# Ten units' q, k and v in one stretch by way of DRAM, two attention units at once, weights in PSUM, adds on GpSimd

## The chip, the cores and the metric

The kernel runs on one core of one Trainium2 chip. The engines that matter here are TensorE (PE in the profile, with its weight loads as PEld), VectorE (DVE), ScalarE (ACT), GpSimd (POOL) and SyncE (SP), which issues every DMA. Each engine works through its own queue in order and waits on semaphores for the others. The metric is the device time of one execution in microseconds (us).

## The reference

x has 2048 rows of 640 numbers, in float32. One layer is computed:

```python
xn = layernorm(x)                                  # over the 640 columns
q, k, v = split(xn @ wqkv)                         # 32 heads of 20 columns each
# sliding, dilated attention: row s sees rows s, s-2, s-4, ... s-14 (8 places)
logits = einsum("bhsd,bhswd->bhsw", q, kg) * 20 ** -0.5   # places before row 0 masked
attn = softmax(logits)
o = einsum("bhsw,bhswd->bhsd", attn, vg)
s = o @ wo
g = silu(((xn @ w_gate) * (xn @ w_up)) @ w_down)   # w_gate, w_up: 640 x 1536
return x + s * g
```

All products are to hold float32 precision.

## The kernel before

Every matrix operand is split into a high and a low part, and a product is the sum of three products of parts (`mm3`, L91, and `ALL3`, L89). ScalarE makes the high part, and VectorE or GpSimd subtracts it from the raw numbers to make the low part (`split`, L84).

The rows are ordered so that 16 tiles of 128 rows hold the even rows first (8 tiles) and then the odd rows (8 tiles): a dilation of 2 becomes two independent halves. Within a half, partition p holds 8 neighbouring rows, so the 8 places that a row sees lie in the same partition or in the one before. k and v of a half are held with 7 extra rows in front (`EXT` = 15), and these are copied from the partition before by DMAs from SBUF to SBUF (L350 to L354).

The attention is cut into twelve **units**: six groups of heads (`GROUPS`: four of five heads, two of six) times the two halves. For a unit, `qkv(u, i)` (L337) computes tile i of its q, k and v: 15 products of 300 or 360 columns into one PSUM bank with the tag q, which has four banks. ScalarE moves the bank's content into the SBUF tiles kv (L348) and q (L349). The tile kv exists twice, one for each half.

`attention(u)` (L357) is the work of a unit on VectorE, written as a generator that hands over after each step with an estimated cost. For each pair of places, q is multiplied with k for two places at once (L380, 1600 or 1920 elements) and summed over the 20 columns of a head (L384). After the mask and the maximum (L388 to L391), ScalarE takes the exponential (L393), and VectorE sums and divides (L396 to L398). Then the weights are multiplied with v, two places at a time (L403), added up (L411), and the two halves of the sum are added into o (L414). SP writes o to DRAM (L419).

TensorE's other large share is the gate and up product. `gate_up(f, ch)` (L440) computes one **piece**: 15 products of 512 columns for gate into a bank with the tag g, 15 for up into a bank u (two banks each). ScalarE moves the gate bank into a tile gs (L451, two of them), VectorE multiplies the up bank with gs into hs (L462), and SP writes hs to DRAM (L466). There are 48 pieces: 12 blocks f of the 1536 columns times 4 chunks ch of 512 rows.

Engines follow the order in which the Python code issues instructions. `advance(budget)` (L424) decides where attention steps stand among TensorE's work: after each q/k/v tile and each half of a piece it gets a budget in estimated microseconds (1.9 or 2.28 for a tile, 3.25 for half a piece) and issues steps of the running generators until the budget is spent. In the main loop (L982) a unit's eight tiles of q, k and v are followed by three pieces; attention of the unit is put in the list after its tiles, and `drain` (L960) issues what is left of the unit before the last one. The weights of a group of heads have one buffer each for the high and low part (wqh, wql); they are replaced after each second unit (`split_wq`, L978, the low part on VectorE). The low parts of the gate and up weights are subtracted on GpSimd, each subtraction put behind a product of the attention (`some_beside`, L145, and `behind`, L151).

After the pieces come the output product of the attention (L830, L96) and the down product (L699), for which o and hs are read back from DRAM.

Of the kernel before, what the change touches and what calls it, by code (L numbers as in the profile page):

```python
# [11 lines left out]
F32 = mybir.dt.float32  # L12
F32R = mybir.dt.float32r
AF = mybir.ActivationFunctionType
# [5 lines left out]
P = 128  # L20
# [31 lines left out]
def kernel(  # L52
# [138 lines left out]

    def idle_product(n):

        nc.tensor.matmul(pt([P, n, P], "q", 4), ident, ident.unsqueeze(1).to_broadcast([P, n, P]), start=True,
                         stop=True)

    for n in (3, 3, 3, 1):
# [67 lines left out]
        for _ in range(len(halves) if n is None else n):  # L265
            halves.pop(0)()

    def trans(s, bank=("q", 4), parts=((0, 4), (4, KD)), later=False):
        hi, lo = xT_tile(s)
        for k0, k1 in parts:  # L270
            p = pt([P, k1 - k0, P], *(("q", 4) if k0 else bank))
# [27 lines left out]

    def spread(s0):  # L300

        p = pt([P, NQ, 2, TPC], "q", 4)
# [15 lines left out]


    UN = [(g, r) for g in range(len(GROUPS)) for r in range(DIL)]  # L320
    q_t, kv_t, kv_buf, kv_zero = {}, {}, {}, {}

    def begin_unit(u):
        g, r = UN[u]
        c = GROUPS[g] * DH
        q_t[u] = st([P, NE, c], "q", 2)
        if r not in kv_buf:
            kv_buf[r] = st([P, EXT * 2 * CMAX], "kv", 2)
            kv_zero[r] = 0
        kv_t[u] = kv_buf[r][:, :2 * EXT * c].rearrange("p (a e c) -> p a e c", a=2, c=c)  # L330
        if kv_zero[r] != GROUPS[g]:
            nc.gpsimd.memset(kv_t[u][0:1, :, 0:W - 1, :], 0.0)
            kv_zero[r] = GROUPS[g]

    ALL_RUNS = [(a, b, k) for a, b in ALL3 for k in range(KD)]

    def qkv(u, i, runs=ALL_RUNS, at=None, act=None):  # L337

        g, r = UN[u]
        c = GROUPS[g] * DH  # L340
        p = pt([P, 3 * c], "q", 4)
        t0 = (i % TPC) * P
        for n, (a, b, k) in enumerate(runs):
            if n == at:
                act()
            nc.tensor.matmul(p, xT[(r * NE + i) // TPC][a][:, k, t0:t0 + P], wq[g][b][:, k], start=n == 0,  # L346
                             stop=n == len(runs) - 1, skip_group_check=act is not None)
        nc.scalar.activation(kv_t[u][:, :, W - 1 + i, :], p[:, c:].rearrange("p (a c) -> p a c", a=2), AF.Copy)  # L348
        nc.scalar.activation(q_t[u][:, i, :], p[:, :c], AF.Copy)  # L349
        for i0, i1 in ((1, 5), (5, NE)):  # L350
            if i == i1 - 1:
                for p0, p1 in ((0, 112), (112, 127)):
                    nc.sync.dma_start(kv_t[u][p0 + 1:p1 + 1, :, i0 - 1:i1 - 1, :],
                                      kv_t[u][p0:p1, :, W - 1 + i0:W - 1 + i1, :])  # L354


    def attention(u):  # L357
        g, r = UN[u]
        nh = GROUPS[g]
        c = nh * DH  # L360
        q, kv = q_t[u], kv_t[u]
        pair, one, small = [(n + 155) / 950 for n in (2 * NE * c, NE * c, NE * nh * W)]
        lg = st([P, NE * nh, W], "lg", 2)
        e = st([P, NE * nh, W], "e", 1)
        yield 1.0

        def places(a, j):

            y = kv[:, a, j:j + NE, :].rearrange("p i c -> p (i c)")
            return bass.AP(y.tensor, y.offset, [y.ap[0], [c, 2], y.ap[1]])  # L370

        def pair_tile():
            return st([P, 2, NE * c], "t", 2)

        def heads(y):
            return y.rearrange("p a (n d) -> p a n d", d=DH)

        for j in PAIRS:
            t = pair_tile()
            nc.vector.tensor_mul(t, q.rearrange("p i c -> p (i c)").unsqueeze(1).to_broadcast([P, 2, NE * c]),  # L380
                                 places(0, j))
            some_beside(t)
            yield pair
            nc.vector.tensor_reduce(out=lg[:, :, j:j + 2].rearrange("p n a -> p a n"), in_=heads(t),  # L384
                                    op=ALU.add, axis=AX.X)
            yield pair
        m0 = lg[0:1].rearrange("p (i h) w -> p i h w", h=nh)
        nc.vector.tensor_add(m0, m0, mask.unsqueeze(2).to_broadcast([1, NE, nh, W]))  # L388
        sm = st([P, 2, NE * nh], "sm", 2)
        nc.vector.tensor_reduce(out=sm[:, 0, :], in_=lg, op=ALU.max, axis=AX.X)  # L390
        nc.vector.tensor_sub(lg, lg, sm[:, 0, :].unsqueeze(2).to_broadcast([P, NE * nh, W]))  # L391
        yield 3 * small
        nc.scalar.activation(e, lg, AF.Exp, scale=SCALE)  # L393
        finish_piece()
        yield small
        nc.vector.tensor_reduce(out=sm[:, 0, :], in_=e, op=ALU.add, axis=AX.X)  # L396
        nc.vector.reciprocal(sm[:, 1, :], sm[:, 0, :])
        nc.vector.tensor_mul(e, e, sm[:, 1, :].unsqueeze(2).to_broadcast([P, NE * nh, W]))  # L398
        yield 3 * small

        def weighted(j, t):
            pw = e[:, :, j:j + 2].rearrange("p n a -> p a n").unsqueeze(3).to_broadcast([P, 2, NE * nh, DH])
            nc.vector.tensor_mul(heads(t), pw, heads(places(1, j)))  # L403

        acc, t = pair_tile(), pair_tile()
        weighted(PAIRS[0], acc)
        yield pair
        for j in PAIRS[1:]:
            weighted(j, t)
            yield pair  # L410
            nc.vector.tensor_add(acc, acc, t)  # L411
            yield pair
        o = st([P, NE, c], "o", 1)
        nc.vector.tensor_add(o.rearrange("p i c -> p (i c)"), acc[:, 0, :], acc[:, 1, :])  # L414
        yield one
# [8 lines left out]
    def advance(budget):  # L424
        credit[0] += budget
        while running and credit[0] > 0:
            try:
                credit[0] -= next(running[0][1])
            except StopIteration:
                running.pop(0)  # L430
        if not running:
            credit[0] = 0

    credit = [0]
# [119 lines left out]
    def out_proj(s, n):  # L554
# [4 lines left out]
        p = pt([P, HALF], "q", 4)  # L559
# [129 lines left out]
    def product(m):  # L689
# [2 lines left out]
        place = "ACACABA"[j]  # L692
        new = j in (0, 1, 5)
        if new:
            bank[place] = pt([P, HALF], {"A": "q", "B": "g", "C": "u"}[place], {"A": 4, "B": 2, "C": 2}[place])
# [122 lines left out]
    def pair_product(p, j):  # L818
        place = "ACACABA"[j]
        new = j in (0, 1, 5)  # L820
        if new:
            bank[p, place] = pt([P, HALF], {"A": "q", "B": "g", "C": "u"}[place], {"A": 4, "B": 2, "C": 2}[place])
# [112 lines left out]
    gate_up(0, 2)  # L935
    trans_q(15)
    low_parts()
    running.append((0, attention(0)))
    for i in range(TPC, NE):
        qkv(1, i)  # L940
        advance(PACE * 1.9)
    running.append((1, attention(1)))
    split_wq(1, nc.gpsimd)
    gate_up(1, 2)
    gate_up(0, 3)
# [11 lines left out]
        if ch == 0:  # L957
            split_wf_beside(f + 1)

    def drain(u):  # L960

        while running and running[0][0] <= u:
            for _ in running.pop(0)[1]:
                pass

    def unit(u):
        drain(u - 2)
        begin_unit(u)
        for i in range(NE):
            if u % 2 and u + 1 < len(UN) and i == 2:  # L970
# [31 lines left out]
    advance(1e9)  # L1002
    split_wo(0)
    split_wo(1)
    load_pair(1)
# [193 lines left out]
```

## Time and profile before

The runs before took 766.74 us (median of three, 766.53 to 766.81). The profiled execution has a span of 765.5 us; its own time is the span and about 1.2 us that lie around it, going by the median.

| engine | busy, us | share of the span |
|---|---|---|
| TensorE, products (PE) | 757.7 | 99% |
| TensorE, weight loads (PEld, beside the products) | 698.8 | 91% |
| VectorE (DVE) | 687.7 | 90% |
| ScalarE (ACT) | 239.1 | 31% |
| GpSimd (POOL) | 123.7 | 16% |

A row of a group of instructions reads: line, engine, operation, output<-input, shape and type of output<-input, count | busy us in total, mean ns of one | idle time of the engine just before, and what ended most of it. The chain of work that ended last is followed back from the last instruction; in order of time its rows are start us, us, engine, tile, line and count. In the waits a row reads: engine, tile and line that waited <- what it waited for: total us, times, longest. In a row of one line's DMAs, the three durations are the least, median and greatest time of the issuing instruction in ns, and the landing is from issue to completion in us. Windows show the busy us of each engine in a stretch.

### The profile page before, as it was taken

The page shows a single profiled execution, that of the slowest core. Times are in us where ns is not written, and L with a number is a line of the kernel's source. Part 1 is how long each engine was busy: PE and PEld are TensorE (multiplying, and loading weights), DVE is VectorE, ACT ScalarE, POOL GpSimd, SP SyncE. Part 2 cuts the span into 40 slices and gives each one's busy share as a digit, 9 for nine tenths or more (in the row PEclk, how much of TensorE's full clock was granted, in tenths as well). Part 3 has the DMA queues.
Part 4 walks back from the last instruction along what each step waited for, and adds up shares of the span by engine and source line. Part 5 has one row for each costly group of instructions (what it writes and reads, how often), then busy time and mean ns, then how long its engine had stood idle before and what let it go on. Part 6 is the DMA issues. An engine that isn't in the chain of part 4 may idle for free.

```text
span 765.5 us, 11301 instructions
## 1 busy us (share of the span) xinstructions
PE 757.7 (99%) x4402; PEld 698.8 (91%) x4402; DVE 687.7 (90%) x748; ACT 239.1 (31%) x539; POOL 123.7 (16%) x147
## 2 busy tenths in 40 slices
PE   8999999999999999999999999999999999999997
PEld 6989889898989899899998989888899999999997
DVE  7899999999998999997999999989988897777775
ACT  4324221130212212211122121023466654444442
POOL 5200311010010100010200000113548900000000
PEclk9999999999999999999999999999999999999999
DMA  8552131331223224304241221355368565555533
GB/s 322 179 192 82 49 84 53 97 93 49 86 67 109 61 62 121 75 29 101 76 120 42 71 76 49 98 148 137 110 207 253 191 252 186 186 186 186 186 104 138
DMA packets 82254, 93.99 MB, mean 123 GB/s; under 512 B 23112, under 2 KB 63384, under 8 KB 82072
## 3 DMA queue, kind: packets, MB, share of 16 engines
q1 hardware_dynamic: 82200, 93.27, 39.2%
q8 instruction: 34, 0.56, 0.3%
q14 instruction: 20, 0.16, 0.1%
HBM read 55.84 MB, written 28.31 MB: 110 GB/s over the span
## 4 chain that ended last, share of the span: by engine, by line
PE 98%; DVE 1%; DMA 1%; SPq 0%; issue 0%; ACT 0%; DVEq 0%
PE q L346 27%; PE g L96 21%; PE u L96 21%; PE q L699 11%; PE u L699 6%; PE q L96 3%; PE q L830 3%; PE g L699 3%; PE u L830 1%; PE g L830 1%; DMA t<-in_xb 1%; DVE wql L87 0%; DVE stats L222 0%; SPq L115 0%; DVE xc L275 0%
## 5 line engine op out<-in xcount | busy, mean ns | idle before, releaser
L96 PE MATMUL g<-xc,wf 128*128 128x512 f32 (+1 forms) x735 | 171.9, 385 | 0.0
L96 PE MATMUL u<-xc,wf 128*128 128x512 f32 (+1 forms) x735 | 171.7, 385 | 0.0
L96 PEld LDWEIGHTS u<-xc,wf 128*128 128x128 f32 x735 | 136.0, 188 | 27.4
L96 PEld LDWEIGHTS g<-xc,wf 128*128 128x128 f32 x735 | 135.5, 188 | 26.6
L346 PE MATMUL q<-wqh,xc 128*128 128x300 f32 (+1 forms) x960 | 157.8, 307 | 1.0 <-DVE rstd L232 1.0
L346 PEld LDWEIGHTS q<-wqh,xc 128*128 128x128 f32 x960 | 144.2, 188 | 2.6 <-DVE rstd L232 1.2
L380 DVE TENSOR_TENSOR t<-q,kv 128x1600 f32<-128x1600 f32 (+1 forms) x48 | 94.2, 1963 | 4.4 <-DMA kv<-kv 4.3
L403 DVE TENSOR_TENSOR t<-e,kv 128x1600 f32<-128x1600 f32 (+1 forms) x48 | 95.6, 2008 | 1.6
L384 DVE TENSOR_REDUCE lg<-t 128x80 f32<-128x1600 f32 (+1 forms) x48 | 92.6, 1930 | 1.2
L451 ACT ACTIVATE gs<-g 128x512 f32<-128x512 f32 x48 | 28.7, 597 | 192.7 <-PE g L96 182.0
L346 PE MATMUL q<-wql,xc 128*128 128x300 f32 (+1 forms) x480 | 85.3, 307 | 0.1
L348 ACT ACTIVATE kv<-q 128x200 f32<-128x200 f32 (+1 forms) x96 | 33.4, 348 | 156.5 <-PE q L346 153.1
L346 PEld LDWEIGHTS q<-wql,xc 128*128 128x128 f32 x480 | 73.5, 188 | 0.3 <-DVE wql L87 0.3
L411 DVE TENSOR_TENSOR t<-t,t 128x1600 f32<-128x1600 f32 (+1 forms) x36 | 70.9, 1969 | 1.0
L699 PE MATMUL q<-xc,wf 128*128 128x320 f32 x432 | 67.3, 309 | 0.0
L699 PEld LDWEIGHTS q<-xc,wf 128*128 128x128 f32 x432 | 64.3, 188 | 0.0
L153 POOL COPY beside<-t 128x1 f32<-128x1 f32 x26 | 4.8, 183 | 362.0 <-DVE t L380 359.8
L462 DVE TENSOR_TENSOR hs<-u,gs 128x512 f32<-128x512 f32 x47 | 32.0, 681 | 3.8 <-PE u L96 2.1
L87 POOL TENSOR_TENSOR xc<-wraw,xc 128x320 fp32r<-128x320 f32 (+1 forms) x22 | 27.4, 1250 | 17.7 <-ACT xc L86 17.7
L143 POOL TENSOR_TENSOR wf<-wraw,wf 128x512 fp32r<-128x512 f32 (+1 forms) x24 | 26.6, 1109 | 0.2 <-issue 0.2
L349 ACT ACTIVATE q<-q 128x100 f32<-128x100 f32 (+1 forms) x96 | 24.5, 256 | 0.0
L662 DVE TENSOR_TENSOR wf<-t,wf 128x768 fp32r<-128x768 f32 x16 | 15.3, 957 | 8.5 <-ACT wf L658 7.8
(264 smaller groups left out, 931.8 us busy)
## 6 DMA issues: line engine op xcount, KB each, us to landing
h_scr<-hs SPq DMA_DIRECT2D x48, 256.0 KB, 2.2
wraw<-in_wgu SPq DMA_DIRECT2D x12, 640.0 KB, 4.5
t<-h_scr SPq DMA_DIRECT2D x8, 768.0 KB, 7.0
hs<-s_scr SPq DMA_DIRECT2D x16, 320.0 KB, 3.7
gs<-in_x SPq DMA_DIRECT2D x16, 320.0 KB, 4.0
out<-q SPq DMA_DIRECT2D x14, 320.0 KB, 2.6
wraw<-h_scr SPq DMA_DIRECT2D x11, 384.0 KB, 5.8
wraw<-in_wd SPq DMA_DIRECT2D x12, 320.0 KB, 4.8
```

Source lines behind the costliest of these rows:

```text
L87: eng.tensor_sub(lo, raw, hi.bitcast(F32))
L96: nc.tensor.matmul(acc, a, b, start=first and n == 0, stop=last and n == len(runs) - 1)
L346: nc.tensor.matmul(p, xT[(r * NE + i) // TPC][a][:, k, t0:t0 + P], wq[g][b][:, k], start=n == 0, stop=n == len(runs) - 1, skip_group_check ...
L348: nc.scalar.activation(kv_t[u][:, :, W - 1 + i, :], p[:, c:].rearrange("p (a c) -> p a c", a=2), AF.Copy)
L380: nc.vector.tensor_mul(t, q.rearrange("p i c -> p (i c)").unsqueeze(1).to_broadcast([P, 2, NE * c]), places(0, j))
L384: nc.vector.tensor_reduce(out=lg[:, :, j:j + 2].rearrange("p n a -> p a n"), in_=heads(t), op=ALU.add, axis=AX.X)
L403: nc.vector.tensor_mul(heads(t), pw, heads(places(1, j)))
L411: nc.vector.tensor_add(acc, acc, t)
L451: nc.scalar.activation(gs, pp[0], AF.Copy)
L462: nc.vector.tensor_mul(hs, pp[1], gs)
L699: nc.tensor.matmul(p, y[:, i, k], wd_t[name][k][:, l], start=new and r == 0, stop=r == len(runs) - 1, skip_group_check=True)
L830: nc.tensor.matmul(b, y, w, start=new and r == 0, stop=r == len(runs) - 1, skip_group_check=True)
```

## The change

- The tag q has three PSUM banks instead of four. The eighth bank goes to a new tag e, which holds the attention weights (the exponentials) of one unit; it was a tile in SBUF.
- Units 0 and 1 are made as before. For units 2 to 11, `qkv` moves each bank with one ScalarE instruction into a staging tile; SP writes four (or three, three and two) tiles of it at a time to a DRAM tensor of the unit. The tiles of these ten units follow each other, with one piece after each second unit (while the next group's weights are made), and the other pieces come after all of them.
- The attention is now one generator for all units, in the order 0, 1, 2, 3, 4, 6, 8, 10, 5, 7, 9, 11. In each turn it does the logits of one unit, and between them the weighted values of the unit before. If the unit to come has not been made, it hands back, and what is left of the budget is dropped.
- q, k and v of a unit are read from DRAM (`load_kq`, `load_kv`: q, then k and its two shifted copies, then v and its two). If the unit is already made this is issued after the o of the previous turn; otherwise when its turn begins.
- The weighted values are taken for one place at a time: VectorE multiplies the weights in PSUM with v (800 or 960 elements), into o for the first place and into one of two tiles for the others, and GpSimd adds these to o. The wide adds on VectorE are gone.
- The q·k product has one tile instead of two in turn.

The diff, without the lines that change only 4 banks to 3:

```diff
     UN = [(g, r) for g in range(len(GROUPS)) for r in range(DIL)]
+    ORDER = [0, 1, 2, 3, 4, 6, 8, 10, 5, 7, 9, 11]
+    def view_kv(u, b):
+        c = GROUPS[UN[u][0]] * DH
+        if b not in kv_buf:
+            kv_buf[b] = st([P, 2, EXT * CMAX], "kv", 2)
+        kv_t[u] = kv_buf[b][:, :, :EXT * c].rearrange("p a (e c) -> p a e c", c=c)
+    def zero_kv(u, b, a):
+        if kv_zero.get((b, a)) != GROUPS[UN[u][0]]:
+            nc.gpsimd.memset(kv_t[u][0:1, a, 0:W - 1, :], 0.0)
+            kv_zero[b, a] = GROUPS[UN[u][0]]
     def begin_unit(u):
+        if u >= DIL:
+            scr[u] = dr.tile([P, 3, NE, c], F32, name=f"qkv_scr_{u}")
+            return
...
+    def load_kq(u):
+        c, b = GROUPS[UN[u][0]] * DH, ORDER.index(u) % 2
+        view_kv(u, b)
+        q_t[u] = st([P, NE, c], "q", 2)
+        nc.sync.dma_start(q_t[u], scr[u][:, 0])
+        load_kv(u, 0)
+    def load_kv(u, a):
+        zero_kv(u, ORDER.index(u) % 2, a)
+        nc.sync.dma_start(kv_t[u][:, a, W - 1:, :], scr[u][:, 1 + a])
+        for p0, p1 in ((0, 112), (112, 127)):
+            nc.sync.dma_start(kv_t[u][p0 + 1:p1 + 1, a, 0:W - 1, :], scr[u][p0:p1, 1 + a, 1:, :])
     def qkv(u, i, runs=ALL_RUNS, at=None, act=None):
-        p = pt([P, 3 * c], "q", 4)
+        p = pt([P, 3 * c], "q", 3)
...
+        if u >= DIL:
+            cuts = (0, 4, NE) if GROUPS[g] == 5 else (0, 3, 6, NE)
+            i0, i1 = next((a, b) for a, b in zip(cuts, cuts[1:]) if a <= i < b)
+            if i == i0:
+                staged[u] = st([P, 3, i1 - i0, c], "ot", 2)
+            nc.scalar.activation(staged[u][:, :, i - i0, :], p.rearrange("p (a c) -> p a c", a=3), AF.Copy)
+            if i == i1 - 1:
+                nc.sync.dma_start(scr[u][:, :, i0:i1, :], staged.pop(u))
+            if i == NE - 1:
+                made.add(u)
+            return
...
-    def attention(u):
+    def attention():
+        twice = st([P, 2, NE * CMAX], "t", 2)
+        terms = st([P, 2, NE * CMAX], "t", 2)
+        before = None
+        for n, u in enumerate(ORDER + [None]):
+            if u is not None:
+                while u not in made:
+                    yield None
...
+                if u >= DIL and u not in q_t:
+                    load_kq(u)
+                    load_kv(u, 1)
...
+            for j in PAIRS:
+                if u is not None:
...
+                    nc.vector.tensor_mul(t, q, k)
+                    some_beside(t)
+                    yield 2 * NE * c * 1.22e-3
+                    nc.vector.tensor_reduce(out=lg[:, :, j:j + 2].rearrange("p n a -> p a n"),
+                                            in_=t.rearrange("p a (n d) -> p a n d", d=DH), op=ALU.add, axis=AX.X)
+                    yield 2 * NE * c * 1.2e-3
+                if before is not None:
+                    for w in (j, j + 1):
+                        cost = values(before, w, terms)
+                        yield cost
+            if before is not None:
+                store_o(before)
+            if u is None:
+                return
+            more = ORDER[n + 1] if n + 1 < len(ORDER) else None
+            if more is not None and more in made and more >= DIL:
+                load_kq(more)
+                load_kv(more, 1)
...
+            e = pt([P, NE * nh, W], "e", 1)
+            nc.scalar.activation(e, lg, AF.Exp, scale=SCALE)
...
+    def values(unit, w, terms):
...
+        t = terms[:, w % 2, :NE * c] if w else y
+        nc.vector.tensor_mul(t.rearrange("p (n d) -> p n d", d=DH),
+                             e[:, :, w].unsqueeze(2).to_broadcast([P, NE * nh, DH]), v)
+        if w:
+            nc.gpsimd.tensor_add(y, y, t)
+        return NE * c * 1.3e-3
...
     def advance(budget):
         credit[0] += budget
         while running and credit[0] > 0:
+            cost = next(running[0], 0)
+            if cost == 0:
+                running.pop()
+            elif cost is None:
+                break
+            else:
+                credit[0] -= cost
+        if credit[0] > 0:
             credit[0] = 0
...
+    piece()
+    for u in range(2, len(UN)):
         begin_unit(u)
         for i in range(NE):
...
-        running.append((u, attention(u)))
         if u % 2 and u + 1 < len(UN):
             split_wq(UN[u + 1][0], nc.vector)
-
-    f0, f1 = KF - 2, KF - 1
-    piece()
-    for u in range(2, len(UN)):
-        unit(u)
-        for _ in range(3 + (u == 2) if u + 1 < len(UN) else len(pieces)):
-            if len(pieces) == 1:
-                load_wf(f1)
             piece()
+    while pieces:
+        if len(pieces) == 1:
+            load_wf(f1)
+        piece()
...
         if ch == 2:
-            drain(len(UN) - 2)
+            advance(1e9)
             load_pair(0)
```

More of the change, by code (lines that the diff above doesn't have):

```diff
@@ L325, in begin_unit @@
         c = GROUPS[g] * DH
+        if u >= DIL:
+            scr[u] = dr.tile([P, 3, NE, c], F32, name=f"qkv_scr_{u}")
+            return
         q_t[u] = st([P, NE, c], "q", 2)
[L327 to L333, printed above, removed]
+        view_kv(u, r)
+        for a in range(2):
+            zero_kv(u, r, a)
+    def load_kq(u):
[9 more added lines that the diff above has]
+            nc.sync.dma_start(kv_t[u][p0 + 1:p1 + 1, a, 0:W - 1, :], scr[u][p0:p1, 1 + a, 1:, :])
     ALL_RUNS = [(a, b, k) for a, b in ALL3 for k in range(KD)]
@@ L354, in qkv @@
                                       kv_t[u][p0:p1, :, W - 1 + i0:W - 1 + i1, :])
-    def attention(u):
-        g, r = UN[u]
[L359 to L415, printed above, removed]
@@ new lines, in attention, with flat @@
+    def attention():
+        def flat(y):
+            return y.rearrange("p i c -> p (i c)")
+        twice = st([P, 2, NE * CMAX], "t", 2)
[5 more added lines that the diff above has]
+                    yield None
+                g, r = UN[u]
+                nh = GROUPS[g]
+                c = nh * DH
+                if u >= DIL and u not in q_t:
+                    load_kq(u)
+                    load_kv(u, 1)
+                q, kv = flat(q_t[u]).unsqueeze(1).to_broadcast([P, 2, NE * c]), kv_t[u]
+                lg = st([P, NE * nh, W], "lg", 2)
+                t = twice.rearrange("p a c -> p (a c)")[:, :2 * NE * c].rearrange("p (a c) -> p a c", a=2)
+            for j in PAIRS:
+                if u is not None:
+                    k = flat(kv[:, 0, j:j + NE, :])
+                    k = bass.AP(k.tensor, k.offset, [k.ap[0], [c, 2], k.ap[1]])
+                    nc.vector.tensor_mul(t, q, k)
[16 more added lines that the diff above has]
+                load_kv(more, 1)
+            m0 = lg[0:1].rearrange("p (i h) w -> p i h w", h=nh)
+            nc.vector.tensor_add(m0, m0, mask.unsqueeze(2).to_broadcast([1, NE, nh, W]))
+            sm = st([P, 2, NE * nh], "sm", 2)
+            nc.vector.tensor_reduce(out=sm[:, 0, :], in_=lg, op=ALU.max, axis=AX.X)
+            nc.vector.tensor_sub(lg, lg, sm[:, 0, :].unsqueeze(2).to_broadcast([P, NE * nh, W]))
+            yield 1.5
+            e = pt([P, NE * nh, W], "e", 1)
+            nc.scalar.activation(e, lg, AF.Exp, scale=SCALE)
+            finish_piece()
+            yield 0.5
+            nc.vector.tensor_reduce(out=sm[:, 0, :], in_=e, op=ALU.add, axis=AX.X)
+            nc.vector.reciprocal(sm[:, 1, :], sm[:, 0, :])
+            nc.vector.tensor_mul(e, e, sm[:, 1, :].unsqueeze(2).to_broadcast([P, NE * nh, W]))
+            yield 1.3
+            before = u, e, st([P, NE, c], "o", 1)
@@ L416, in attention, with store_o @@
+    def store_o(unit):
+        u, _, o = unit
+        g, r = UN[u]
+        c = GROUPS[g] * DH
         for b in range(NQ):
@@ L937 @@
     low_parts()
-    running.append((0, attention(0)))
+    made.add(0)
+    running.append(attention())
     for i in range(TPC, NE):
@@ L941 @@
         advance(PACE * 1.9)
-    running.append((1, attention(1)))
+    made.add(1)
     split_wq(1, nc.gpsimd)
@@ L958, in piece @@
             split_wf_beside(f + 1)
[L960 to L967, printed above, removed]
+    f0, f1 = KF - 2, KF - 1
+    piece()
+    for u in range(2, len(UN)):
         begin_unit(u)
```

27 lines of the change are left out of this document (13 added, 14 removed).

## The prediction

> **What bounds the kernel now.** I read the page first (busy shares, then the chain), then the chain in order of time, then the windows, and last the groups of VectorE (DVE) and GpSimd (POOL).
>
> ```profile
> span 765.5 us, 11301 instructions
> ...
> PE 757.7 (99%) x4402; PEld 698.8 (91%) x4402; DVE 687.7 (90%) x748; ACT 239.1 (31%) x539; POOL 123.7 (16%) x147
> ...
> PE 98%; DVE 1%; DMA 1%; SPq 0%; issue 0%; ACT 0%; DVEq 0%
> ```
>
> TensorE is the chain: 98% of it, busy 99%. A saving on any other engine buys nothing unless TensorE waits for that engine. What matters is what the change could make TensorE wait for. The chain in order of time gives the yardstick:
>
> ```profile
> 71.58 8.20 PE q L346 x60
> 79.78 3.40 PE g L96 x15
> 83.19 3.40 PE u L96 x15
> 106.98 16.40 PE q L346 x120
> 413.78 19.20 PE q L346 x120
> ```
>
> One q/k/v tile costs TensorE 8.20/4 = 2.05 us (five heads) or 19.20/8 = 2.40 (six heads), one gate/up piece 6.80. The windows show who is nearly as busy:
>
> ```profile
> core 0: us, PE busy (x) PEld busy (x) DVE busy (x) ACT busy (x) POOL busy (x), PEclk, DMA share, GB/s
> 100.00:150.00 50.00, 50.00 (x270) 44.20 (x269) 48.77 (x37) 8.60 (x23) 3.78 (x6) 1.00 0.29 82
> ```
>
> While attention runs, DVE is at 48.77 of 50, so there is little room for it to become late. It can hold TensorE up in three ways: the gate/up banks and gs tiles are freed by DVE's product hs, the weight halves wql come from DVE, and ScalarE runs Exp (which needs DVE's logits) in the same queue that empties the q banks.
>
> **The change, part by part.** Durations of one instruction:
>
> ```profile
> L380 DVE TENSOR_TENSOR t<-q,kv x48: 1814/1818/3518, 73.7 to 491.2; 128x1600 f32<-128x1600 f32 x32, 128x1920 f32<-128x1920 f32 x16
> ```
> ```profile
> L384 DVE TENSOR_REDUCE lg<-t 128x80 f32<-128x1600 f32 x32 | 58.2, 1819 | 0.8
> L384 DVE TENSOR_REDUCE lg<-t 128x96 f32<-128x1920 f32 x16 | 34.4, 2152 | 0.4
> L411 DVE TENSOR_TENSOR t<-t,t 128x1600 f32<-128x1600 f32 x24 | 43.8, 1823 | 0.7
> L414 DVE TENSOR_TENSOR o<-t 128x800 f32<-128x800 f32 x8 | 7.9, 990 | 0.2
> L414 DVE TENSOR_TENSOR o<-t 128x960 f32<-128x960 f32 x4 | 4.6, 1158 | 0.1
> L462 DVE TENSOR_TENSOR hs<-u,gs 128x512 f32<-128x512 f32 x47 | 32.0, 681 | 3.8 <-PE u L96 2.1 <-issue 1.7
> L715 DVE TENSOR_TENSOR q<-e,u 128x320 f32<-128x320 f32 x8 | 3.9, 488 | 3.8 <-PE u L699 3.8
> L391 DVE TENSOR_TENSOR lg<-lg,sm 128x320 f32<-128x320 f32 x8 | 3.9, 492 | 0.3
> L391 DVE TENSOR_TENSOR lg<-lg,sm 128x384 f32<-128x384 f32 x4 | 2.2, 559 | 0.1
> L87 DVE TENSOR_TENSOR wql<-wraw,wqh 128x900 fp32r<-128x900 f32 x2 | 2.2, 1088 | 0.0
> L143 POOL TENSOR_TENSOR wf<-wraw,wf 128x512 fp32r<-128x512 f32 x16 | 20.7, 1295 | 0.2 <-issue 0.2
> ```
> ```profile
> DVE sm L396 <- ACT e L393: 8.4, 8, 2.5
> ```
>
> *DVE work.* A five-head unit before: 12 wide products and reduces at 1.82, three wide adds at 1.82, one add at 0.99, six softmax steps of about 0.48, and 1.05 waiting for Exp (8.4/8): 32.2 us. After: the adds are gone and the value products are eight of 800 elements. Nothing in the trace reads a broadcast from PSUM; the nearest are L462 and L715, with one PSUM operand, whose line gives 0.97 at 800 and 1.13 at 960, beside 0.99 and 1.16 for SBUF alone (L414). So 8x1.82 + 8x0.97 + 2.9 + 1.05 = 26.3 us; six heads 8x2.15 + 8x1.13 + 3.3 + 1.05 = 30.6. Over 8 and 4 units that is 333 us against 409: DVE is relieved of 76 us. TensorE was not waiting for them, so they are worth nothing by themselves.
>
> *The adds on GpSimd.* 84 adds of 800 or 960 elements, both operands in SBUF. The rows below (320 elements 0.88) and L143 (512 elements 1.30) give 1.92 and 2.26 us each. Per unit that is 13 to 16 us of a queue with time to spare. But the two engines hold each other up:
>
> ```profile
> 81.23 5.16 POOL L87 TENSOR_TENSOR wql<-wraw,wqh 128x900 fp32r<-128x900 f32 x2 [56.28 <-ACT wqh L86]
> 81.52 3.52 DVE L380 TENSOR_TENSOR t<-q,kv 128x1600 f32<-128x1600 f32 x1
> 85.07 1.82 DVE L384 TENSOR_REDUCE lg<-t 128x80 f32<-128x1600 f32 x1
> ```
> ```profile
> 586.00 0.88 POOL L87 TENSOR_TENSOR xc<-wraw,xc 128x320 fp32r<-128x320 f32 x1
> 586.10 1.13 DVE L602 TENSOR_TENSOR lg<-wraw 128x320 f32<-128x320 f32 x1
> 586.84 1.13 POOL L87 TENSOR_TENSOR xc<-lg,xc 128x320 fp32r<-128x320 f32 x1
> ```
>
> The q·k product, with both operands in SBUF, takes 3.52 instead of 1.82 when it starts behind a GpSimd subtraction, while the reduce beside the rest of that work keeps 1.82. At 586 the DVE operation gets in between two GpSimd operations: they take turns. The value products read their weights from PSUM and escape (L462 shows no such stretching); the q·k products, the mask add and the subtraction of the maximum do not. In each pair DVE runs product, reduce, value product, value product; the add of the first value product starts 0.97 before the next q·k product is due, which therefore waits 1.92 - 0.97 = about 1.0. That happens before two products of a unit and before the mask add, and the subtraction waits 1.4 for the last add: 4.4 us a unit, 5.3 with six heads. The lower end is zero (every add falls under reduces and hs), the upper 1.92 more for each product if GpSimd goes first: 8 us a unit. I take 4.4, because the rows show turns.
>
> *q, k, v through DRAM.* 24 stores and 70 loads come on SP's queue, 40 shifts within SBUF go (54 rows more). ScalarE does one eviction a tile instead of two, cheaper and off the path. The loads of the next unit are issued after the o store, which waits for GpSimd's last add, and the next q·k product waits for q, k and two shifted copies of k.
>
> ```profile
> L353 SPq DMA_DIRECT2D kv<-kv x48: 621/820/998, 38.6 to 473.7; - x48
> ...
> DMA to landing us min/median/max: 2.4/3.1/5.8
> ```
> ```profile
> t<-h_scr SPq DMA_DIRECT2D x8, 768.0 KB, 7.0
> ...
> o_scr<-o SPq DMA_DIRECT2D x4, 400.0 KB, 4.1
> ```
>
> From the last value product (T): last add done T+3.4, o store issued T+4 to T+4.4, four loads of 1.15 MB by T+6, landed (between the 4.1 of 400 KB and the 7.0 of 768 KB queued in twos, from the first issue) T+9 to T+11. DVE's softmax with its port waits ends at T+6.3. So DVE idles 2.5 to 5 us at such a boundary; I take 3.5 for seven of them. Units 2, 8 and 10 are reached before their q, k, v are made: their loads start only after the last store has landed (4 us), so DVE can go on about 8 us after TensorE has finished that unit. [...] No run here shows these loads yet.
>
> *Banks.* q has three banks for four. In steady work an eviction takes under 0.5 of each 2.05 us: nothing. At the start the second q/k/v tile now waits for the first one's eviction: at most 1 us.
>
> **The sum.** Attention steps are handed out by estimated costs, 344 us in all, against 0.93 to 0.96 us for each us of TensorE; so they are spread over 385 us of TensorE work (30 pieces 204, 80 tiles 175, three tiles of unit 1 6), after forfeiting 19 while units are not made. Without new waits DVE needs 333 + 30 hs at 0.68 + four splits at 1.8 = 361 and fits. With them, by stretch:
> - units 2, 3, 4, 6 (TensorE 122 us): DVE starts 8 late, needs 4x30.7 + three boundaries 10.5 + hs and splits 7.5 = 141. Late by 27. TensorE can run three tiles ahead (three banks, Exp blocking the fourth): 6. It loses 21.
> - unit 8: DVE has 37 us of work in 45 and recovers, then waits for unit 10's loads, 8 late again.
> - units 10, 5, 7, 9, 11 and the last values (TensorE 168 us): q·k 81, values 52, softmax and Exp 21, port waits 25, boundaries 14, hs 16, last adds alone on GpSimd 5: 214. Late by 8 + 46 = 54; TensorE can run three half pieces ahead: 10. It loses 44.
>
> From then on DVE has only hs and TensorE is unhindered, so nothing is won back. 765.5 + 65 = 830.5 in terms of the profiled execution; the median, 766.7, lies 1.2 above the span, so I predict 831 us.
>
> **Rivals.**
> - *Not slower.* The adds and loads hide: 361 us of DVE work in 385. It decides at (385 + 10 - 361)/11 = 3 us of new waits per unit; below that the time is 766 to 768. For it: the 76 us relief and DVE's idle time after attention. Against it: the 3.52 row and the o store ahead of the loads.
> - *Half the waits.* Ports alone without boundaries, or the reverse, take 25 to 40 us off the 65: 785 to 805.
> - *GpSimd goes first at the port.* 1.92 more before about 2.2 products a unit, 11 units: 45 us more, 876. Against it the turn-taking at 586.
> - *The adds become the bound*, so the relief is not had: 7x1.92 = 13 us plus the weight subtractions against over 30 of DVE a unit; only for the last unit, counted above.
>
> **How the numbers follow.** Main case 0.57 (its own range 805 to 860), half the waits 0.19, GpSimd first 0.12, not slower 0.12. The range 775 to 882 leaves out most of the last and little else. From the same cases, with 0.2% (1.5 us) as what can be told from no change: slower 0.88, same 0.08, faster 0.04, as TensorE's idle time before is 765.5 - 757.7 = 8 us, all of it start and drain.
>
> **What would show it.** TensorE below 95% in the slices of attention and waiting for DVE (hs) and ScalarE (q); the q·k product's mean above 2.3 us against reduces at 1.82; SP's o store waiting for POOL and DVE's q·k product for DMA; DVE busy share falling late, after attention. Wrong if DVE's q·k products stay at 1.82, if the loads land before softmax ends, or if value products with PSUM weights are dearer than 1.0 us: each 0.1 there adds 9.6 us of DVE work over the 96 products.

## The result, and the profile after

The changed kernel takes 880.77 us (median of four runs, 879.95 to 881.32); the kernel before took 766.64 beside it. The ratio is 1.149, with a 95% interval of 1.147 to 1.150. The forecast was 831 us, so the loss is 114 us where 64 were expected: the direction was right, the size little more than half. The time lies 1 us inside the top of the stated range (775 to 882) and above the main case's own (805 to 860).

The page of the profiled execution: busy shares, the span in 40 slices for TensorE and DVE, and the largest group.

```profile
span 879.1 us, 11410 instructions
...
PE 784.7 (89%) x4402; PEld 716.4 (81%) x4402; DVE 651.7 (74%) x748; ACT 233.1 (27%) x459; POOL 345.9 (39%) x236
...
PE   8989998797869959959387939989999999999997
...
DVE  7899876796969590979786949611268889787775
...
L466 POOL TENSOR_TENSOR o<-o,t 128x800 f32<-128x800 f32 (+1 forms) x84 | 218.5, 2601 | 149.7 <-DVE t L463 134.8
```

TensorE is no longer always busy (89%, before 99%). Both rows of slices have their holes between slice 7 and slice 27, which is while attention runs; after that TensorE is at 9 up to the last slice, and DVE falls to 1, 1 and 2 before the work of the end comes. The windows of the kernel before and of the kernel after, cut where TensorE has done the same products, put a number on it (busy us of each engine, number of instructions, granted clock, DMA share, GB/s):

```profile
62.00:472.10 410.10, 410.10 (x2269) 371.50 (x2268) 390.42 (x305) 88.98 (x242) 37.32 (x47) 1.00 0.27 75
472.10:765.50 293.40, 289.12 (x1792) 275.99 (x1790) 244.23 (x285) 125.94 (x234) 70.68 (x59) 1.00 0.52 169
```
```profile
62.00:584.00 522.00, 435.44 (x2268) 388.08 (x2267) 399.42 (x331) 83.56 (x164) 261.62 (x137) 0.91 0.37 112
584.00:879.10 295.10, 290.71 (x1798) 277.24 (x1796) 199.80 (x261) 126.07 (x232) 68.47 (x56) 1.00 0.51 165
```

The same work of some 2,270 products takes 522.0 us instead of 410.1. That is 111.9 of the 113.6 us by which the span grew, and nothing is won back behind it (295.1 against 293.4). In this stretch DVE has 399.4 us of work in 522, so it is idle for 122.6, and TensorE is idle for 86.6; the other 25.3 us of TensorE's loss are products that take longer (435.4 against 410.1), which the last section takes up. The waits of the kernel after say for what (total us, times, longest):

```profile
DVE t L421 <- DMA kv<-qkv_scr: 90.8, 10, 20.8
ACT e L446 <- DVE lg L443: 74.4, 10, 12.7
...
PE g L96 <- POOL wf L143: 39.6, 6, 14.4
...
PE q L374 <- DVE wql L87: 22.7, 4, 10.0
...
PE u L96 <- DVE hs L523: 10.1, 3, 8.1
...
PE q L374 <- ACT ot L381: 7.2, 2, 6.3
```

Ten times, once for each unit that comes from DRAM, the q·k product waits for k: 90.8 us of DVE's 122.6. TensorE waits in turn for DVE (wql, hs), for ScalarE whose Exp waits for DVE (ot), and most of all for wf, the low parts of the gate and up weights, which GpSimd makes. One boundary between two units shows how these hang together. The timeline from 419 us of the kernel after (start, duration, instruction, idle time before it and what ended it):

```profile
418.95 4.73 POOL L466 TENSOR_TENSOR o<-o,t 128x960 f32<-128x960 f32 x2 [0.16 <-DVE t L463]
...
423.71 0.36 SPq L477 DMA_DIRECT2D o_scr<-o  x1
...
424.12 0.57 SPq L353 DMA_DIRECT2D q<-qkv_scr  x1
...
425.50 0.50 DVE L451 TENSOR_TENSOR e<-e,sm 128x320 f32<-128x320 f32 x1
425.78 0.97 SPq L361 DMA_DIRECT2D kv<-qkv_scr  x2
...
427.24 0.96 SPq L361 DMA_DIRECT2D kv<-qkv_scr  x2
...
432.39 1.82 DVE L421 TENSOR_TENSOR t<-q,kv 128x1600 f32<-128x1600 f32 x1 [6.39 <-DMA kv<-qkv_scr]
...
434.28 0.18 POOL L153 COPY beside<-t 128x1 f32<-128x1 f32 x1 [9.38 <-DMA h_scr<-hs]
434.42 1.26 POOL L143 TENSOR_TENSOR wf<-wraw,wf 128x512 fp32r<-128x512 f32 x1
...
435.74 1.22 PE L96 MATMUL g<-xc,wf 128*128 128x512 f32 x2 [11.52 <-POOL wf L143]
```

The last value product of the unit before ends at 419.87. SP cannot issue the o store before GpSimd's last add is done (423.71), and the loads stand behind the store. DVE has finished the softmax at 426.00 and is idle until q and k have landed, 8.3 us after the first load was issued. The low parts on GpSimd are placed behind that same q·k product (`behind`, the COPY at 434.28), so TensorE, which needs them, has stood still for 11.52 us, since 424.22: it stops before DVE does.

DVE's own groups are about where the prediction had them. Groups of the kernel after:

```profile
L421 DVE TENSOR_TENSOR t<-q,kv 128x1600 f32<-128x1600 f32 x32 | 73.0, 2281 | 43.9 <-DMA kv<-qkv_scr 43.9
...
L463 DVE TENSOR_TENSOR t<-e,kv 128x800 f32<-128x800 f32 x56 | 53.0, 980 | 0.0
L463 DVE TENSOR_TENSOR t<-e,kv 128x960 f32<-128x960 f32 x28 | 31.5, 1150 | 5.5 <-POOL o L466 5.5
L440 DVE TENSOR_TENSOR lg<-lg,mask 1x320 f32<-1x320 f32 x8 | 11.9, 1487 | 0.0
L443 DVE TENSOR_TENSOR lg<-lg,sm 128x320 f32<-128x320 f32 x8 | 11.8, 1472 | 0.3
```

### The profile page after: what moved, and what is told of

The parts are those of the page before. It is cut to its first block, busy times and chain, and to the rows that moved or that the text cites. A ratio compares the mean times of both kernels' runs of the same rounds, so it can differ in the third digit from the quotient of the medians.

```text
span 879.1 us, 11410 instructions
## 1 busy us (share of the span) xinstructions
PE 784.7 (89%) x4402; PEld 716.4 (81%) x4402; DVE 651.7 (74%) x748; ACT 233.1 (27%) x459; POOL 345.9 (39%) x236
## 5 line engine op out<-in xcount | busy, mean ns | idle before, releaser
L466 POOL TENSOR_TENSOR o<-o,t 128x800 f32<-128x800 f32 (+1 forms) x84 | 218.5, 2601 | 149.7 <-DVE t L463 134.8
L96 PE MATMUL g<-xc,wf 128*128 128x512 f32 (+1 forms) x735 | 175.5, 389 | 39.6 <-POOL wf L143 39.6
L96 PE MATMUL u<-xc,wf 128*128 128x512 f32 (+1 forms) x735 | 180.0, 398 | 10.1 <-DVE hs L523 10.1
L421 DVE TENSOR_TENSOR t<-q,kv 128x1600 f32<-128x1600 f32 (+1 forms) x48 | 115.9, 2414 | 90.8 <-DMA kv<-qkv_scr 90.8
L374 PE MATMUL q<-wqh,xc 128*128 128x300 f32 (+1 forms) x960 | 165.5, 317 | 15.6 <-ACT ot L381 7.2
L96 PEld LDWEIGHTS u<-xc,wf 128*128 128x128 f32 x735 | 142.0, 196 | 40.9 <-DVE hs L523 11.3
L374 PEld LDWEIGHTS q<-wqh,xc 128*128 128x128 f32 x960 | 151.0, 195 | 18.5 <-ACT ot L381 7.9
L374 PEld LDWEIGHTS q<-wql,xc 128*128 128x128 f32 x480 | 77.0, 195 | 24.6 <-DVE wql L87 24.5
L463 DVE TENSOR_TENSOR t<-e,kv 128x800 f32<-128x800 f32 (+1 forms) x84 | 84.5, 1037 | 5.5 <-POOL o L466 5.5
L381 ACT ACTIVATE ot<-q 128x300 f32<-128x300 f32 (+1 forms) x80 | 34.4, 441 | 157.2 <-PE q L374 138.1
L87 POOL TENSOR_TENSOR wql<-wraw,wqh 128x300 fp32r<-128x300 f32 (+2 forms) x6 | 8.4, 1420 | 59.7 <-ACT wqh L86 59.7
L446 ACT ACTIVATE e<-lg 128x320 f32<-128x320 f32 (+1 forms) x12 | 5.5, 458 | 74.4 <-DVE lg L443 74.4
```

What stands on the lines that cost most here:

```text
L87: eng.tensor_sub(lo, raw, hi.bitcast(F32))
L96: nc.tensor.matmul(acc, a, b, start=first and n == 0, stop=last and n == len(runs) - 1)
L381: nc.scalar.activation(staged[u][:, :, i - i0, :], p.rearrange("p (a c) -> p a c", a=3), AF.Copy)
L421: nc.vector.tensor_mul(t, q, k)
L463: nc.vector.tensor_mul(t.rearrange("p (n d) -> p n d", d=DH), e[:, :, w].unsqueeze(2).to_broadcast([P, NE * nh, DH]), v)
L466: nc.gpsimd.tensor_add(y, y, t)
```

## The experiments

Three theories of why the loss was 114 and not 64 us. A: the wait for the loads at each boundary, set by where they are issued. B: DVE's work, drawn out by GpSimd's adds at the port, as the prediction calls what makes the two engines hold each other up (what it is no run shows; measured are the longer instructions, 2.28 us for a q·k product of five heads that most often took 1.82 before). C: the low parts on GpSimd, which stand behind the q·k product. Each experiment is one run, but for the version with all three edits, which has four.

**Loads of q and k earlier.** q, k and k's copies of the next unit are issued after the second pair of places instead of after the o store; v stays.

```diff
                     yield 2 * NE * c * 1.2e-3
+                    if more is not None and more in made and more >= DIL and more not in q_t and j > 0:
+                        load_kq(more)
...
-                load_kq(more)
+                if more not in q_t:
+                    load_kq(more)
                 load_kv(more, 1)
```

> q and k of the next unit are loaded half a turn earlier (their buffers are free since the turn before), v where it was. Theory A, the loads behind the o store are the main cause: VectorE's 91 us of waiting for DMA fall below 30 and the time to about 815 us. Theory B, the port between VectorE and GpSimd is the main cause: VectorE is late anyway, the waits move elsewhere, 860 us or more.

It took 837.1 us, 44 less, where theory A had about 815. The waits of this kernel:

```profile
DVE t L427 <- DMA kv<-qkv_scr: 44.4, 3, 21.3
```

Seven of the ten waits are gone, and with them 46.4 us of DVE's idle time. The three that remain (11.9, 11.3 and 21.3 us) are those of units 2, 8 and 10, whose tiles are not made yet when DVE gets to them. A holds for the seven, but not as the whole cause: 70 us of loss remain.

**Loads ahead of the o store.** All seven loads stand in SP's queue at the end of a turn, as they did, but before the store and not behind it.

```diff
-            if before is not None:
-                store_o(before)
             if u is None:
+                store_o(before)
                 return
             more = ORDER[n + 1] if n + 1 < len(ORDER) else None
             if more is not None and more in made and more >= DIL:
                 load_kq(more)
                 load_kv(more, 1)
+            if before is not None:
+                store_o(before)
```

> The change with SP's order turned round at each turn's end: the seven loads of the next unit, then the o store. If the loads are late because they stand behind a store that waits for GpSimd's last add (3.8 us after VectorE's last value product), VectorE's wait at the seven plain boundaries falls by about that, 25 us in all, and the time to 850 to 860 us. If the loads' own transfer time is what counts, less than 10 us.

835.9 us, 45 less, more than expected and as much as the earlier loads gave; in both runs q and k no longer stand behind the store. The waits of this kernel, and the boundary before unit 5 from its timeline:

```profile
DVE t L421 <- DMA kv<-qkv_scr: 44.4, 5, 20.7
```
```profile
358.69 0.51 SPq L353 DMA_DIRECT2D q<-qkv_scr  x1
...
366.43 1.82 DVE L421 TENSOR_TENSOR t<-q,kv 128x1600 f32<-128x1600 f32 x1 [1.25 <-DMA kv<-qkv_scr]
```

Two of the five waits are of 1.25 and 0.68 us; the rest are again units 2, 8 and 10. The seven plain boundaries cost 47.7 us of DVE in the kernel after (5.82 to 8.46 each) and 1.9 here. What uncovered the loads was one wait on SP's queue: the store's, for GpSimd's last add. More comes off than that wait is long, because SP, with no store in front, issues q and k as soon as it gets to them: 0.6 to 18.6 us before DVE's last value product ends, where the kernel after issues them 4 us behind it. In the boundary shown it is 0.6 us (the product ends at 359.30), and there the softmax does not quite cover the loads.

**Attention at a slower pace.** `PACE` scales the budget that each tile and half piece gives to attention steps. With 0.8 the steps are spread over more of TensorE's work.

```diff
-PACE = 1.0
+PACE = 0.8
```

> The budget constant goes from 1.0 to 0.8, so the same attention steps are spread over about 480 us of TensorE work instead of 385. If TensorE loses because VectorE needs more time than the steps' estimated costs say (A and B alike), VectorE has the room it lacks and the time falls to 800 to 835 us. If the loss is fixed latencies that TensorE meets wherever the steps stand, it stays above 865 us.

837.2 us, 43.5 less, just above the expected range.

```profile
DVE t L421 <- DMA kv<-qkv_scr: 64.9, 10, 7.6
```

Now all ten waits are of the plain kind, 6.5 us on average; the long ones, for units not made, are gone. The pace also gives DVE more of TensorE's time for the same steps, so this run does not price those three waits alone.

**Both.** Loads of q and k earlier, and `PACE` at 0.85.

> Early q and k, and the budget constant at 0.85 (steps spread over about 450 us of TensorE work). VectorE's work without the waits for loads, about 31 us a unit and hs, then fits: 780 to 800 us, with TensorE waiting mainly where units 2, 8 and 10 are reached before they are made. If it stays above 830 us, lateness of VectorE is not what TensorE pays for.

789.8 us, as expected. The two gains nearly add, though the second was measured at a pace of 0.8: 880.8 - 43.7 - 43.5 = 793.6. Its waits:

```profile
PE g L96 <- POOL wf L143: 14.5, 5, 7.5
...
DVE t L427 <- DMA kv<-qkv_scr: 7.6, 2, 5.8
```

DVE hardly waits for loads now, and TensorE's largest wait is for the low parts on GpSimd.

**Low parts not behind the q·k product.** In the kernel after, the subtractions of the gate and up weights are issued on GpSimd at once.

```diff
-            beside.append((f, lambda k=k: nc.gpsimd.tensor_sub(lo[:, k], raw[:, k], hi[:, k].bitcast(F32))))
+            nc.gpsimd.tensor_sub(lo[:, k], raw[:, k], hi[:, k].bitcast(F32))
```

> The low parts of the gate and up weights are subtracted on GpSimd as soon as they can be, not each behind a q.k product. Theory C, TensorE's 40 us of waiting for them are a cause of their own: these waits go and the time falls to about 840 us. Theory A or B (VectorE is late, and this queue only passes it on): the waits move to hs and wql, 865 us or more.

874.5 us, only 6 less. The waits:

```profile
DVE t L421 <- DMA kv<-qkv_scr: 91.6, 10, 20.0
...
PE u L96 <- DVE hs L523: 43.0, 9, 8.2
```

TensorE's 39.6 us of waiting for wf are gone and its wait for hs has grown from 10.1 to 43.0. While DVE is late, wf is one of several ways in which TensorE learns of it; taking that way off leaves the next. C is not a cause of its own here.

**All three.** Earlier q and k, `PACE` 0.85, low parts at once.

> Early q and k, budget constant 0.85, and the low parts of the gate and up weights not hung behind a q.k product. If the 14.5 us that TensorE still waits for those in the run with the first two edits are a cause of their own once VectorE is in time: 772 to 780 us. If they only pass on VectorE's lateness: 786 to 792 us. Neither theory has it below 766, where TensorE's products alone end.

771.97 us (four runs, 770.47 to 772.13), a ratio of 1.006 to the kernel before (1.004 to 1.008). Once DVE is on time, the same edit of the low parts that gave 6 us gives 18 (789.8 to 772.0). C is a cause of its own then, presumably because a subtraction placed behind a q·k product comes late at a slower pace even if that product waits for nothing. The page of this kernel:

```profile
span 770.4 us, 11378 instructions
...
PE 760.0 (99%) x4402; PEld 700.4 (91%) x4402; DVE 651.8 (85%) x748; ACT 233.8 (30%) x459; POOL 350.4 (45%) x219
```

DVE is 36 us less busy than before the change and the kernel is no faster, because TensorE's 760 us are the chain again. No version that was run beats the kernel before.

**No adds.** GpSimd's additions of the weighted values are left out.

```diff
-            nc.gpsimd.tensor_add(y, y, t)
```

> GpSimd's adds are left out, so o holds only the first of eight weighted values; all else stays. Theory B (port): the q.k product falls to 1.82 and 2.15 us, mask add and subtraction to 0.5, about 4 us a unit, and with the stalls behind them the time to 820 us or less. Theory A (loads): the o store is free about 3 us sooner but so is softmax, waits for DMA stay above 60 us, time 840 us or more.

814.9 us, 66 less. Groups of this kernel:

```profile
L421 DVE TENSOR_TENSOR t<-q,kv 128x1600 f32<-128x1600 f32 x32 | 58.1, 1817 | 27.2 <-DMA kv<-qkv_scr 27.1
...
L421 DVE TENSOR_TENSOR t<-q,kv 128x1920 f32<-128x1920 f32 x16 | 34.4, 2152 | 42.6 <-DMA kv<-qkv_scr 42.6
...
L443 DVE TENSOR_TENSOR lg<-lg,sm 128x320 f32<-128x320 f32 x8 | 3.9, 493 | 0.3
...
L440 DVE TENSOR_TENSOR lg<-lg,mask 1x320 f32<-1x320 f32 x8 | 3.8, 470 | 0.0
```

Without the adds the three operations that read SBUF twice are at their old durations, so the difference is the price of the port: 23.3 us for the q·k products, 12.3 for the masks and 12.6 for the subtractions of the maximum, all shapes together 48.2 us, or 4.4 for each of the 11 turns with values. DVE's waits for the loads also fall by 21 us (90.8 to 69.7); the o store has no add to wait for here. B is real, and of the size that the prediction gave it; it isn't the missing part.

**No adds and earlier loads.**

> Both at once: q and k loaded half a turn earlier, and GpSimd's adds left out (o holds the first of eight weighted values). If loads and port are two causes that add up, 44 and 66 us come off together, less the clock's share counted twice, and the time is 770 to 785 us; what is left are the waits for units 2, 8 and 10 to be made. If they are one cause (each hides the other), it stays near the 815 us of the run without adds.

794.2 us, above the expected range: apart the two edits gave 66 and 44 us, together 87, as each of them also shortens the waits for the loads. DVE still waits for loads four times, 53.2 us in all, and TensorE has holes of 5.2 us at 151 and 4.9 at 284, before low halves of the q/k/v weights that DVE makes. With neither port waits nor plain boundaries, 27 us of loss remain, and what DVE waits for is almost all units not yet made.

**Adds on VectorE.** The change, with its additions moved from GpSimd to DVE.

```diff
-            nc.gpsimd.tensor_add(y, y, t)
+            nc.vector.tensor_add(y, y, t)
```

> The change with its adds on VectorE instead of GpSimd: no port waits, but 84 adds of about 1.0 and 1.16 us more on VectorE, 88 us, against about 48 us of port waits saved. If VectorE's work in the stretch is what counts, this is slower than the change: 890 to 915 us. If GpSimd's adds hurt by more than their port waits (the o store and the weight subtractions queue behind them), it is faster: below 870 us.

891.4 us. The q·k product is back at 1.83 us there, but 84 adds of about 1 us are DVE's. Giving them to GpSimd is worth 10.7 us within this change.

**The value part alone.** The kernel before (its order, its copies within SBUF, one unit at a time) with only the weights in PSUM, three q banks, values for one place at a time and the adds on GpSimd.

> The kernel before, with only the value part changed: weights in PSUM, one place at a time, adds on GpSimd, three q banks; no DRAM, the old order of units and pieces, steps handed out by the old formula of costs (27 us a unit instead of 34). If the port is a cause that needs no loads, VectorE needs 26.3 + 4.4 us for 27 us of budget plus hs, TensorE waits a little in each unit: 770 to 785 us. If port waits alone are harmless because three pieces follow each unit and VectorE catches up there: 766 to 768 us.

820.4 us: missed by far, for a reason that the expectation did not have. Its waits:

```profile
DVE t L407 <- POOL o L410: 65.8, 59, 3.8
...
DVE t L379 <- DMA kv<-kv: 62.3, 9, 10.7
```

Eight value products in a row (0.99 us each) run at the rate of GpSimd's adds (2.00): 59 of the 84 products that GpSimd adds wait for one of the two tiles. What hides the adds in the change is the logits of the next unit in between, that is, two units at once (there these waits are 5.5 us in all). The prediction's rival "the adds become the bound" is false for the change and true for this part of it. The q·k product of five heads is 1.87 here, as hardly any adds run beside it. The 62.3 us of waiting for k's copies come with it; what part of the 820 they are was not separated.

**Weights in SBUF.** The change with e in SBUF again, and four q banks.

```diff
-    p = pt([P, 3 * c], "q", 3)
+    p = pt([P, 3 * c], "q", 4)
...
-            e = pt([P, NE * nh, W], "e", 1)
+            e = st([P, NE * nh, W], "e", 1)
```

> The change with the weights in SBUF again and four q banks; the adds stay on GpSimd. If the port holds any VectorE operation with two SBUF operands, each value product now waits for the add before it, some 1.0 us for seven of a unit, 77 us more of VectorE: 930 us or more, and the value product's mean goes from 0.98 to about 1.8 us. If PSUM is not what spared the value products: 875 to 885 us, the mean stays; the one 2.65 us gap at 63 us (three q banks) goes in both cases.

908.7 us, 28 more, between the two expectations. Groups of this kernel:

```profile
L421 DVE TENSOR_TENSOR t<-q,kv 128x1600 f32<-128x1600 f32 x32 | 81.4, 2544 | 39.9 <-DMA kv<-qkv_scr 39.8
...
L463 DVE TENSOR_TENSOR t<-e,kv 128x800 f32<-128x800 f32 x56 | 57.6, 1062 | 0.0
L421 DVE TENSOR_TENSOR t<-q,kv 128x1920 f32<-128x1920 f32 x16 | 48.9, 3056 | 45.9 <-DMA kv<-qkv_scr 45.9
L463 DVE TENSOR_TENSOR t<-e,kv 128x960 f32<-128x960 f32 x28 | 36.6, 1327 | 12.2 <-POOL o L466 12.2
...
L440 DVE TENSOR_TENSOR lg<-lg,mask 1x320 f32<-1x320 f32 x8 | 16.1, 2012 | 0.0
```

The value products themselves lengthen little (0.98 to 1.06, 1.15 to 1.33); the adds behind them end later (2.52 to 2.77 us each for five heads), and it is the next q·k products (2.28 to 2.54, 2.68 to 3.06) and the masks (1.49 to 2.01) that pay. So the place in PSUM does what the prediction said of it (with PSUM weights the product takes 980 ns beside the adds and the same 980 in the run without adds; 1150 and 1147 with six heads), and more than the value product's own row tells.

## Why the prediction was right or wrong

Right:

- *Direction and mechanism.* DVE becomes late in attention, TensorE waits for it, and nothing is won back: 111.9 of the 113.6 us lie in that stretch.
- *The durations.* Value product 0.97 and 1.13 predicted, 0.98 and 1.15 measured; the last unit's adds, alone at the end of attention, 2.26 predicted for six heads and 2.26 measured (mean of the seven from 561 us on). Over all turns the adds are longer, 2.52 and 2.76 on average, where the prediction had 1.92 and 2.26.
- *Port waits.* 4.4 us a unit predicted (5.3 with six heads); measured, for five heads 4x0.46 at the products, 1.02 at the mask and 0.98 at the subtraction, 3.8 in all, and over all turns 4.4. That is the size of engines that take turns; the rival in which GpSimd goes first would have had 8 us a unit. Its 876 us come closest to the 881 by luck.
- *The softmax's end*, T + 6.3 predicted, T + 6.1 at 420 us.

Wrong, by the terms of the sum:

- *"Landed T+9 to T+11 ... I take 3.5 for seven of them".* They landed at T + 12.5 and the seven waits are 6.8 us on average: 47.7 instead of 24.5. The end was taken from two loads in a row (768 KB in 7.0 us). Here the store, q, three loads of k and three of v stand on the queue together, about 2.3 MB, and took 8.3 us from the first load to k's landing; in the longer boundary of six heads (shown below) the DMA engines are 90% busy at 218 GB/s. The prediction counted the four loads that DVE waits for, not the three of v and the store, which are under way at the same time. In the run with q and k earlier, where they go without v and the store, the four of a five-head unit take 5.8 to 6.4 us from the first issue to the last landing, within the prediction's 4.1 to 7.0 (10.6 once, right behind unit 10's loads); in the kernel after they take 7.3 to 9.5. A load of 400 KB of k or v lands 4.9 us after its issue there and 6.2 in the kernel after (medians).
- *"About 8 us late" for units 2, 8 and 10.* DVE starts them some 11 us after TensorE has finished them (unit 10: last tile evicted at 341.21, DVE at 351.76), and it comes to unit 10 long before that. They cost DVE 11.5, 10.7 and 20.8 us of idle time: 43.0, where three times 8 would be 24. Rows of the timeline around unit 10:

```profile
317.33 3.76 DVE L87 TENSOR_TENSOR wql<-wraw,wqh 128x1080 fp32r<-128x1080 f32 x2
...
320.32 1.87 PE L374 MATMUL q<-wql,xc 128*128 128x360 f32 x5 [10.04 <-DVE wql L87]
...
351.76 2.16 DVE L421 TENSOR_TENSOR t<-q,kv 128x1920 f32<-128x1920 f32 x1 [20.83 <-DMA kv<-qkv_scr]
```

  The low half of unit 10's weights stands in DVE's queue behind attention steps that were late, so TensorE begins that unit 10 us late; DVE then comes to the unit at 330.9, before its tiles are done, and waits for TensorE and the loads. The prediction did not have lateness go from DVE to TensorE and back to DVE. Here it is paid twice, once on each side.
- *"TensorE can run three half pieces ahead: 10".* It could not. Of TensorE's 86.6 us of idle time 39.6 are waits for wf and 10.1 for hs. wf was listed nowhere among the ways in which DVE can hold TensorE up, although its subtractions were said to stand behind products of the attention. At 424.22 TensorE stops for wf before DVE, busy until 426.00, has anything to wait for. The run with the low parts issued at once was 6 us faster.
- *"At the start the second q/k/v tile now waits ...: at most 1 us".* The wait for three banks is elsewhere, and 2.36 us: at 63.44, because ScalarE's evictions stand behind an `xc` copy (L316) that waits for DVE. The row of the kernel after:

```profile
65.80 0.96 PE L374 MATMUL q<-wqh,xc 128*128 128x300 f32 x5 [2.36 <-ACT q L388]
```

  With four q banks (the run with the weights in SBUF) this wait is absent, and it is the only hole of over 1 us that TensorE has left in the 772 us version once it has started (2.37).

Added up: 65 + 23 (boundaries) + 19 (units not made) + 6 (no running ahead by way of wf) + 2 (bank) = 115, less 4 for port waits taken slightly too high, is 111 against 113.6 measured. These terms are read from different runs and are not independent, some are idle time of DVE and not of TensorE, the sum has the 8 us for units 2 and 10 only, and the 25.3 us of longer products have no term; so this is an account of sizes, no proof, and a part of the agreement is luck. What the runs show by themselves is that the order of store and loads is worth 45 us, that early loads and a slower pace are worth 91 together, and with the low parts freed 109 of the 114. How the pace's share divides between the waits for units not made and DVE's port waits stays open.

## What to carry to other kernels

When a step is moved to a slower engine (here an add of 800 elements, 0.99 us on VectorE and 2.52 on GpSimd), look at what is queued behind the instruction that waits for its last result: here a store in front of seven loads cost 45 us, and a swap of a few lines took it back. Price a load by all that stands on the queues with it, not by its own bytes: here the same four loads took 7.3 to 9.5 us with the store and v, and 5.8 to 6.4 without. And when an engine off the chain becomes late, list every way in which the bounding engine depends on it (buffers, weights made on a third engine behind it, evictions queued with its work): closing one of them changed little here until the lateness itself was gone (6 us, and then 18).

## What the runs showed of the hardware

The clock was not in the prediction at all. Windows of the kernel after around its longest hole, columns as above:

```profile
506.00:521.00 15.00, 0.86 (x4) 0.38 (x2) 6.43 (x7) 0.49 (x1) 3.15 (x5) 0.69 0.90 218
521.00:524.00 3.00, 2.77 (x7) 2.20 (x8) 3.00 (x3) 1.32 (x2) 0.17 (x1) 0.50 0.31 127
524.00:530.00 6.00, 6.00 (x25) 4.90 (x24) 3.33 (x4) 0.55 (x1) 2.25 (x1) 0.88 0.15 46
```

The hole is of 14.4 us, from 506.86 to 521.23. In windows of 1 us the clock is 1.00 up to 511, 0.50 from 512 to 525 and 1.00 again from 526: it fell some 5 us into the hole and came back some 4 us after the products had begun again. At 0.50 they follow each other at 0.427 us instead of 0.227. The first up half behind the hole, from the timeline of the kernel after, takes 5.29 us, where the next half, at 526.94, takes 3.56:

```profile
521.82 5.29 PE L96 MATMUL u<-xc,wf 128*128 128x512 f32 x15
```

In all, TensorE is busy 27.0 us longer (784.7 against 757.7) for the same products, and its clock over the stretch is 0.91. How much of the 114 us this is was not settled: in the stretch DVE is the late engine and does not wait for TensorE's up products (none of its waits there ends on one), so slow products fill time in which TensorE would otherwise have waited. Where DVE waits for units not yet made, they would lengthen that wait; no run separates the two.
